# A scheduled RWKV-and-MLP kernel: four buffers of gated values for three, and its list of steps in another order

## The chip, the cores and the metric

The kernel runs on one core of a Trainium2 chip. The metric is the device time of one execution in microseconds (us). The engines have short names here, as in the profile: PE is TensorE (matmuls; PEld is its loading of weights), DVE is VectorE, ACT is ScalarE, POOL is GpSimd, and SP is SyncE, which only issues DMAs. POOL and ACT issue DMAs as well.

## The reference

A linear attention with a decaying state (4 sequences, 8 heads, 768 steps, head size 48) feeds a two-layer MLP with a leaky ReLU (3072 tokens, width 384, inner width 2048). Inputs and output are float32.

```python
for t in range(S):
    kt, vt, rt = (k[:, :, t].copy(), v[:, :, t].copy(), r[:, :, t].copy())
    cur = np.einsum('bhd,bhe->bhde', u[None] * kt, vt)
    y[:, :, t] = np.einsum('bhd,bhde->bhe', rt, state + cur)
    state = w[None, :, :, None] * state + np.einsum('bhd,bhe->bhde', kt, vt)
...
h = x @ w_in
g = np.maximum(0.01 * h, h)
return (g @ w_out).astype(np.float32)
```

## The kernel before

The 3072 tokens are 24 tiles of 128 tokens (n = 0 to 23; six tiles make a sequence). The recurrence is computed tile by tile: inside a tile as a masked product of scores, between the tiles of a sequence through a state. Two tiles make a block (m = 0 to 11) for the MLP.

**The list.** Nothing in the code decides on an order at run time. ORDER (L33) is one string of some 890 step names. The loop at L810 walks it, and each name calls a function that adds one operation to its engine's stream; every engine runs its own steps in the order in which they stand in the list. Sched (L83) works out from what each operation reads and writes which semaphores it waits for. So a step that waits holds up all that stand behind it on the same engine, whether they need it or not. `@` and digits after a name give the PSUM banks that the step opens; a bank can be opened again when its last reader is done.

The steps that are spoken of here, a letter and the number of a tile n or of a block m:

- `k`, `r`, `v` n (L271): load of a tile by POOL, from float32 in DRAM to bf16; `i`, `w`: load of a quarter of the MLP's weights in and out; `p1`: table u; `p9`: a ramp from which the masks are made; other `p`: tables and constants at the start; `p21`: the matmul that spreads w for the tables.
- `P` n (L394): DVE multiplies r and k by tables of powers of w, into qk. `T` n.half (L414): PE transposes it for tiles 0 to 7, and `C` (ACT, L428) copies it out to tp; from tile 8 on `X` n (SP, L408) does it by a DMA transpose.
- `D` (DVE, L434) for tiles 0 to 5, `E`, `f`, `R` (DVE, L439, L445, L450) from tile 6 on: the diagonal term u. `L` n (POOL, L465) lays it into the tile's at buffer by a select.
- `A` n (PE, L473): scores of a tile, into two banks. `M`, `m`, `N` (DVE, ACT, DVE; L487 to L515): mask, into at.
- `K` n (PE, L527): sum of keys times values. `V` (DVE, L557): the diagonal term times v, tiles 0 to 5. `B`, `W` (DVE, L565, L576): the next state st.
- `Y` n (PE, L581): the tile's output. `O` n (ACT, L624): into xT.
- `G` (PE, L633) and `g` (ACT, L648): first MLP product and gate for one tile, four times in block 0. `J` m.j (PE, L656) and `j` m.j (ACT, L670): the same for both tiles of a block and two of 16 column blocks; six matmuls of 256 columns and one activation into gT.
- `t`, `b` (DVE, L707, L719): sums of w_out quarters and of gT blocks. `Z` m.k (PE, L748): one of seven products of eight matmuls of 192 columns each that make the second MLP product of a block from these sums. `z` m.k (ACT or DVE, L772): what is taken out of its bank, added up, into out_sb. `o` n (L696): store of a tile.
- `F` (PE, L382): one filler matmul that nobody reads, in the first 11 us; `q`: a memset.

**Rings.** RINGS (L25) gives the number of buffers of each kind. Its seventh entry, NG, is that of gT, the gated values of a block (L217): block m uses gT[m % NG], and j m.j waits until all readers of the former block in that buffer (its Z and b steps) are done. k and r have ten buffers each, and so has v.

**Where it stands.** The attention runs ahead of the MLP. The first J begins when tiles 0 to 3 are through; from there on J and Z steps make up most of PE's stream, and the attention's steps of later tiles stand between them.

Of the kernel before, what the change touches and what calls it, by code (L numbers as in the profile page):

```python
# [11 lines left out]
B, H, S, D = 4, 8, 768, 48  # L12
L = 128
# [4 lines left out]
E = 64  # L18
# [6 lines left out]
RINGS = (6, 8, 6, 6, 6, 3, 3, 8, 10, 10)  # L25
# [18 lines left out]
f7 J1.5@0 R6 O5 R7 j1.1 K6@7 L6 A7@23 B6 j1.5 A6@45 J2.6@6 j1.4 L7 M6 J2.1@7 k10 J0.5@0 M7 j2.1 J2.4@1 k11 j0.5
b1.0 Y6@7 j2.4 r10 Y7@0 b0.0 J2.5@5 O7 v8 b0.1 O6 J2.7@4 j2.6 b1.1 r11 J2.3@7 j2.7 J2.0@6 j2.5 k13 t0 j2.3
J2.2@0 j2.0 Z0.0@7 b1.2 j2.2 P9 Z0.1@1 z0.0 t1 X9 Z1.0@0 b2.0 J3.1@2 b0.3 Z0.2 P8 Z1.1@3 z0.2 z1.0 t2 X8 z0.1
Z0.3@4 j3.1 J3.3@5 E9 E8 Z0.4 k18 P10 j3.3 f8 K7@6 z1.1 Z1.2 t3 X10 k12 J3.2@2 z1.2 B7 r12 Z1.3@5 f9 E10 r15
z0.4 Z0.5 W7 P11 J3.6@6 r18 f10 X11 z0.5 Z0.6 b1.3 v16 Z1.4 R8 j3.6 E11 J3.7@1 L8 R9 J3.5@6 z1.3 j3.7 R10 r14
# [117 lines left out]
def bass_rwkv5_eagle__then__act_leaky_relu_kernel(  # L166
# [60 lines left out]
    add = sch.add  # L227
# [43 lines left out]
    def load_one(which, n):  # L271
        b, c = divmod(n, NC)
        t0 = c * L
# [596 lines left out]
```

## Time and profile before

| | |
|---|---|
| three runs | 165.57, 164.47, 164.97 us |
| median | 164.97 us |
| profiled execution, its own time | 165.07 us |
| its span, first to last instruction | 163.3 us |
| granted TensorE clock, mean | 1.000 |

| engine | busy us | share of the span | instructions |
|---|---|---|---|
| PE | 154.8 | 95% | 2299 |
| PEld | 137.6 | 84% | 2299 |
| DVE | 130.5 | 80% | 260 |
| ACT | 88.2 | 54% | 194 |
| POOL | 88.1 | 54% | 101 |

Busy time of PE counts a matmul from its start to a modelled end, so that matmuls overlap, and the mean of a matmul in a table of groups is longer than the distance between two. The distance is what PE's time is made of. In the lines of the chain of waits, the second number is the time that the chain spends there, which for back-to-back instructions is that distance.

The busy share in 40 slices of 4.1 us each shows where the engines work; the last line is the share of the DMA engines, in tenths:

```profile
PE   5959999999999698999999999999999999999993
...
DVE  2678978979989999999999999999867770561552
ACT  3486686979443334722795528359057454637120
POOL 7999999996079958999974229223032000000000
...
DMA  6999999999999999999999999900261000005025
```

DVE has hardly a free tenth from 45 to 110 us, the DMA engines until 107 us. POOL's work is for the most part the issuing of loads.

### The profile page before, as it was taken

What the parts mean: (1) busy time and instruction counts of PE and PEld (TensorE: products, weight loads), DVE (VectorE), ACT (ScalarE), POOL (GpSimd) and SP (SyncE); (2) the same over time, 40 slices, a digit from 0 to 9 for tenths busy, and PEclk for the clock granted to TensorE, in tenths of its full rate; (3) what the DMA queues carried; (4) which work ended last, traced back from release to release, by engine and by line L of the source; (5) the groups of instructions that cost most, each with busy time, mean ns of one, the idle gap of its engine ahead of it and who ended that gap; (6) DMA issues with size and microseconds to landing.
All of it is one profiled execution on the core that took longest, in us unless ns stands there. A gap on an engine that the chain in (4) does not pass through costs nothing.

```text
span 163.3 us, 5367 instructions
## 1 busy us (share of the span) xinstructions
PE 154.8 (95%) x2299; PEld 137.6 (84%) x2299; DVE 130.5 (80%) x260; ACT 88.2 (54%) x194; POOL 88.1 (54%) x101
## 2 busy tenths in 40 slices
PE   5959999999999698999999999999999999999993
PEld 1737888888999587999898998989989999999992
DVE  2678978979989999999999999999867770561552
ACT  3486686979443334722795528359057454637120
POOL 7999999996079958999974229223032000000000
PEclk9999999999999999999999999999999999999999
DMA  6999999999999999999999999900261000005025
GB/s 105 137 167 167 154 174 163 186 204 144 145 121 161 100 151 152 130 145 87 150 131 211 264 128 151 230 4 0 62 199 52 0 4 0 0 18 180 4 98 193
DMA packets 100234, 19.89 MB, mean 122 GB/s; under 512 B 93169, under 2 KB 100210, under 8 KB 100210
## 3 DMA queue, kind: packets, MB, share of 16 engines
q0 software_dynamic: 75616, 10.03, 93.8%
q1 hardware_dynamic: 23266, 9.12, 30.4%
q10 hardware_dynamic: 1328, 0.39, 1.0%
q8 instruction: 18, 0.29, 0.7%
q14 instruction: 6, 0.05, 0.1%
HBM read 20.65 MB, written 4.72 MB: 155 GB/s over the span
## 4 chain that ended last, share of the span: by engine, by line
PE 60%; POOL 21%; DVE 9%; DMA 6%; issue 2%; POOLq 0%; DVEq 0%
PE ps_all L766 28%; PE ps_all L664 25%; POOL rk_sb L284 11%; DMA rk_sb<-in_r_dram 6%; POOL v_sb L284 4%; PE ps_all L609 3%; PE ps_all L481 2%; POOL w_out_sb L300 2%; POOL w_in_sb L296 2%; DVE qk L399 2%; DVE at L505 2%; POOL at L467 1%; PE ps_all L539 1%; DVE out_sb L787 1%; DVE s_tok L452 1%
## 5 line engine op out<-in xcount | busy, mean ns | idle before, releaser
L673 ACT ACTIVATE gT<-ps_all 128x512 bf16<-128x512 f32 x92 | 52.0, 604 | 29.3 <-PE ps_all L766 14.1
L664 PE MATMUL ps_all<-xT,w_in_sb 128*128 128x256 bf16 x552 | 66.6, 273 | 0.5 <-DVE at L505 0.5
L664 PEld LDWEIGHTS ps_all<-xT,w_in_sb 128*128 128x128 bf16 x552 | 52.4, 98 | 7.3 <-DVE at L505 0.8
L467 POOL TENSOR_SCALAR_AFFINE_SELECT at<-s_tok 128x1024 bf16<-128x1024 f32 x18 | 20.6, 1155 | 27.0 <-DVE s_tok L452 26.9
L766 PE MATMUL ps_all<-tw,gs 128*128 128x192 bf16 x288 | 28.3, 246 | 0.1
L735 DVE TENSOR_TENSOR gs<-gT 128x1024 bf16<-128x1024 bf16 x24 | 16.1, 686 | 11.1 <-ACT gT L673 5.8
L284 POOL DMA_DIRECT2D rk_sb<-in_k_dram x23 | 21.0, 918 | 7.2 <-DVE ku L442 6.4
L766 PEld LDWEIGHTS ps_all<-tw,gs 128*128 128x128 bf16 x288 | 24.0, 98 | 0.4 <-issue 0.3
L505 DVE CAST_PREDICATED at<-mask,ps_all 128x1024 bf16<-128x1024 uint16 x18 | 21.5, 1216 | 2.0 <-PE ps_all L481 1.8
L284 POOL DMA_DIRECT2D v_sb<-in_v_dram x23 | 21.1, 923 | 0.6 <-PE ps_all L539 0.6
L284 POOL DMA_DIRECT2D rk_sb<-in_r_dram x23 | 21.3, 932 | 0.0
L766 PE MATMUL ps_all<-w_out_sb,gT 128*128 128x192 bf16 x192 | 19.8, 246 | 0.0
L787 DVE TENSOR_TENSOR out_sb<-ps_all,snap 128x192 f32<-128x192 f32 x37 | 12.6, 351 | 5.9 <-PE ps_all L766 5.8
L627 ACT ACTIVATE xT<-ps_all 128x384 bf16<-128x384 f32 x24 | 11.0, 494 | 11.5 <-PE ps_all L609 10.3
L777 ACT ACTIVATE snap<-ps_all 128x192 f32<-128x192 f32 x36 | 11.1, 338 | 11.3 <-PE ps_all L766 10.3
L766 PEld LDWEIGHTS ps_all<-w_out_sb,gT 128*128 128x128 bf16 x192 | 16.1, 98 | 0.5
L399 DVE TENSOR_TENSOR qk<-rk_sb,tab 128x768 bf16<-128x768 bf16 x23 | 13.9, 611 | 2.9 <-DMA rk_sb<-in_r_dram 2.7
L609 PE MATMUL ps_all<-at,v_sb 128*32 128x128 bf16 x384 | 10.4, 220 | 1.1 <-DVE vs L560 1.1
L432 ACT ACTIVATE tp<-ps_all 128x512 bf16<-128x512 f32 x16 | 9.0, 596 | 3.9 <-PE ps_all L421 3.6
L609 PEld LDWEIGHTS ps_all<-at,v_sb 128*32 128x32 bf16 x384 | 8.0, 96 | 3.1 <-DVE vs L560 1.4
L766 PE MATMUL ps_all<-w_out_sb,gs 128*128 128x192 bf16 x96 | 9.9, 246 | 0.0
L782 ACT ACTIVATE out_sb<-ps_all 128x192 f32<-128x192 f32 x11 | 3.7, 332 | 11.3 <-PE ps_all L766 11.3
(69 smaller groups left out, 196.6 us busy)
## 6 DMA issues: line engine op xcount, KB each, us to landing
out_dram<-out_sb SPq DMA_DIRECT2D x22, 192.0 KB, 2.8
rk_sb<-in_k_dram POOLq DMA_DIRECT2D x23, 96.0 KB, 6.0
rk_sb<-in_r_dram POOLq DMA_DIRECT2D x23, 96.0 KB, 6.0
v_sb<-in_v_dram POOLq DMA_DIRECT2D x23, 96.0 KB, 5.5
w_in_sb<-in_moe_w_in_dram POOLq DMA_DIRECT2D x4, 384.0 KB, 6.4
w_out_sb<-in_moe_w_out_dram POOLq DMA_DIRECT2D x4, 384.0 KB, 11.1
tp<-qk SPq DMA_TRANSPOSE x16, 5.2
out_sb<-in_k_dram ACTq DMA_DIRECT2D x1, 192.0 KB, 2.8
```

The lines of the kernel that those rows point to most:

```text
L284: add("pool", lambda: G.dma_start(dst, src), W=[key], dma=f"{which}{n}")
L399: add("dve", lambda: V.tensor_tensor(qk[iq][:, :, 0:D], both, by, ALU.mult), R=[("r", n % NRK), ("k", n % NRK), "qtab", "ktab", ("qk0", iq ...
L467: add("pool", lambda: G.affine_select(out=at[ia][:, :, :, :].rearrange("p two m i -> p (two m) i"), in_=s_tok[i2][:, :].unsqueeze(2).to_br ...
L505: add("dve", lambda: V.copy_predicated(dst, mask[:, :].bitcast(mybir.dt.uint16).unsqueeze(1).to_broadcast([128, H, 128]), raw), R=keys + [ ...
L609: last = PE.matmul(ps_y[32 * q:32 * q + 32, 128 * s:128 * s + 128], a, m, start=first_mm and (s == 0 or whole), stop=last_mm and whole)
L627: add("act", lambda: A.activation(xT[m % NX][:, :, 128 * half:128 * half + 128], ps[i][:, 0:HD].rearrange("p (s t) -> p s t", t=128), AF.C ...
L664: last = PE.matmul(ps[i][:, 256 * f:256 * f + 256], w_in_sb[:, s, 128 * fb:128 * fb + 128], xT[ix][:, s, :], start=s == 0, stop=s == NSL - 1)
L673: add("act", lambda: A.activation(gT[ig][:, 2 * j:2 * j + 2, :].rearrange("p f t -> p (f t)"), ps[i][:, :], AF.Prelu, alpha=0.01), R=[key] ...
L735: add(eng, lambda: on.tensor_tensor(x[i][:, :, :], a, b, op), R=keys, W=[("gs", m % 2, i)])
L766: done = PE.matmul(ps[i][:, 0:NH], lhs[:, s, :], rhs[:, s, :], start=bool(opens) and s == 0, stop=s == HF - 1, skip_group_check=not (opens ...
L777: add("act", lambda: A.activation(snap[i2][j][:, :], ps[i][:, 0:NH], AF.Copy), R=[key], W=[("snap", i2, j)])
L787: add("dve", lambda: V.tensor_tensor(out_sb[io][:, cols], ps[i][:, 0:NH], snap[i2][j][:, :], ALU.add), R=[key, ("snap", i2, j), *after], W ...
```

## The change

NG goes from 3 to 4. A set PAIRED appears, which is empty; load_one can now load two tiles in one DMA for the tiles in that set, and for the others it builds the same pattern from a view with one dimension more. ORDER is replaced: the same steps with the same numbers, but for the fillers (12 instead of 21), in another order and with other banks.

```diff
 VHW = {0}
-RINGS = (6, 8, 6, 6, 6, 3, 3, 8, 10, 10)
+PAIRED = set()
+RINGS = (6, 8, 6, 6, 6, 3, 4, 8, 10, 10)
...
-        t0 = c * L
-        src = {"k": k, "r": r, "v": v}[which][b].rearrange("h t d -> t h d")[t0:t0 + L, :, :]
-        if which == "v":
-            dst = v_sb[:, n % NV, :].rearrange("p (h e) -> p h e", e=E)[:, :, 0:D]
-        else:
-            dst = {"k": k_sb, "r": r_sb}[which][:, n % NRK, :].rearrange("p (h d) -> p h d", d=D)
-        key = (which, n % (NV if which == "v" else NRK))
+        m, slots = (2 if n in PAIRED else 1), (NV if which == "v" else NRK)
+        i = n % slots
+        src = {"k": k, "r": r, "v": v}[which][b].rearrange("h (c t) d -> t c h d", t=L)[:, c:c + m, :, :]
+        dst = {"k": k_sb, "r": r_sb, "v": v_sb}[which][:, i:i + m, :]
+        dst = dst.rearrange("p c (h e) -> p c h e", e=E if which == "v" else D)[:, :, :, 0:D]
+        if m == 1:
+            src, dst = src[:, 0, :, :], dst[:, 0, :, :]
...
-            add("pool", lambda: G.dma_start(dst, src), W=[key], dma=f"{which}{n}")
+            add("pool", lambda: G.dma_start(dst, src), W=[(which, i + j) for j in range(m)], dma=f"{which}{n}")
```

Of the list, which is 44 lines long, these are the stretches that the text speaks of, sorted by engine. POOL, from the start to the last load ahead of L12:

```
before: k1 k2 p9 r1 r2 i1 r3 k3 v1 k5 r5 v2 i0 v3 r4 k4 k7 r7 i3 v4 k6 r6 i2 v7 p1 v5 v6 w0 w1 w3 w2
        k9 r9 v9 r13 k8 r8 L6 L7 k10 k11 r10 v8 r11 k13 k18 k12 r12 r15 r18 v16 L8 r14 v12 L9 k15 L10
        r16 L11 v13 v18 v14 k14 v19 v10 k16 k17 v11 r19
after:  p9 k2 r2 k3 r3 r1 k1 v1 i1 r5 k5 v2 i0 v3 k4 r4 k7 r7 i3 p1 v4 k6 r6 i2 v5 v7 v6 w3 w2 w0 w1
        r9 k9 k8 r8 L6 L7 k10 r10 k13 r11 r13 v13 k11 v8 k20 v9 r15 k12 r12 k15 L8 L9 L10 v15 k18 v16
        L11 k14 v12 v10 r16 k16 v11 r14 r18 k17
```

and, behind L12 and L13, before `k19 k21 v15 r17 k20 v22 r20 r22 v20 r23 v21 L14 r21 k22 L15 L18`, after `k21 k23 v21 k19 r20 r17 k22 r19 v18 L14 L15 r22 L18`.

DVE at the start, from P0.0:

```
before: P0.0 P0.1 P1 P2 p32 D0 M0.1 M0.0 V0 B0 P3 D1 N1.1 M1.0 V1 B1 D2 P5 D3 M3.0 V2 M2 B2 V3 M3.1 P4 M5.0
after:  P0.0 p15 P0.1 p31 P2 D0 P3 q4 p32 M0.1 P1 M0.0 B0 V0 D1 M1.0 q5 N1.1 V1 P5 D2 B1 M2 V2 D3 B2 M3.0
        M3.1 V3 P4 B3 D5 P7 W3 M5.0
```

and from the first t to M10:

```
before: t0 b1.2 P9 t1 b2.0 b0.3 P8 t2 E9 E8 P10 f8 t3 B7 f9 E10 z0.4 W7 P11 f10 z0.5 b1.3 R8 E11 R9 z1.3
        R10 z0.3 P13 f11 B8 z1.4 M8 M9 W8 z1.5 P12 R11 E12 E13 M10
after:  t0 P9 P8 t1 b1.3 P10 t3 E9 E10 P13 f9 f10 b2.0 t2 B7 E8 R9 f8 E11 P11 f11 R8 W7 R10 B8 z0.5 z0.4
        z1.3 z0.3 z1.4 M8 M9 W8 E12 R11 P12 z1.5 M10
```

PE at the start, to the first J:

```
before: F1.256.10@0 F1.256.2@1 p21@7 F1.512.18@6 F1.128.8@5 F1.256.1@6 F1.128.28@0 F1.128.18@1 F1.256.9@2
        F1.256.15@3 F1.256.12@4 F1.128.24@5 F1.256.6@6 F1.256.0@7 F1.512.1@0 F1.256.17@1 T0.0@0 F1.128.25@7
        F1.256.8@6 F1.512.15@7 F1.128.9@1 T0.1@2 F1.512.8@3 T1.1@4 A0@01 T2.1@5 T2.0@6 F1.256.16@7 T1.0@3
        K0@2 Y0@7 A1@01 A2@23 T3.1@4 T3.0@1 K1@5 G0.1@6 Y1@7 A3@01 K2@4 T5.1@5 T5.0@7 G1.1@0 G1.0@7 K3@5
        G0.0@0 Y2@6 Y3@4 T4.1@7 A5@01 T4.0@6 J1.0@2
after:  F1.512.6@0 F1.128.27@1 p21@0 T0.1@7 F1.256.15@6 T0.0@5 F1.512.4@6 F1.512.9@7 T2.1@6 F1.128.30@7
        A0@01 T2.0@7 F1.256.18@2 T3.0@3 F1.512.11@4 F1.512.1@5 T1.1@4 K0@2 T1.0@1 T3.1@0 A1@45 K1@6 Y0@7
        A2@45 Y1@2 G0.1@7 T5.1@1 F1.128.20@0 K2@2 G1.1@6 T5.0@0 F1.128.28@1 F1.128.18@5 A3@34 G0.0@1 G1.0@5
        K3@2 Y2@1 Y3@0 A5@34 T4.0@1 T4.1@2 J1.1@7
```

and from the first Z to the first J4:

```
before: Z0.0@7 Z0.1@1 Z1.0@0 J3.1@2 Z0.2 Z1.1@3 Z0.3@4 J3.3@5 Z0.4 K7@6 Z1.2 J3.2@2 Z1.3@5 Z0.5 J3.6@6 Z0.6
        Z1.4 J3.7@1 J3.5@6 J3.4@5 K8@1 J3.0@7 A8@45 A9@12 Z1.5 Z2.0@6 Z1.6 Y8@4 Y9@5 A10@01 A11@23 Z3.0@7
        J4.4@4 J4.3@5 J4.7@0
after:  Z0.0@5 J2.2@4 Z0.1@3 J3.3@2 J3.4@4 J3.2@0 J3.0@7 J3.1@6 Z1.0@4 Z0.2 Z1.1@0 Z1.2 Z0.3@1 Z0.4 Z0.5
        K8@2 Z1.3@6 Z1.4 A9@23 A8@67 Z1.5 Z1.6 Z0.6 Z2.0@1 Y8@7 Y9@6 A10@23 A11@45 Z3.0@7 J4.6@6 J4.7@0
```

SP's transposes run in the order 9 8 10 11 12 13 15 14 17 18 16 21 22 19 20 23 before, and 8 9 10 11 13 12 15 16 14 21 18 17 22 19 20 23 after; the stores stand between them in both.

More of the change, by code (lines that the diff above doesn't have):

```diff
@@ L44 @@
[L44 to L48, printed above, removed]
@@ new lines @@
+A7@01 L6 j1.4 A6@34 R7 J0.5@5 j0.4 L7 j0.7 M6 J1.5@7 j0.5 J2.1@6 k10 j1.5 M7 K6@2 J2.0@5 r10 J2.6@7 B6 k13 b0.0
+Y6@4 j2.6 Y7@3 b1.0 r11 J2.4@0 O7 b0.1 O6 J2.5@7 r13 j2.0 b1.1 K7@1 j2.4 J2.7@2 b0.2 v13 b0.3 J3.5@0 j2.7 k11 t0
+J2.3@3 j3.5 v8 J3.7@2 P9 j2.3 J3.6@0 j3.7 Z0.0@5 j2.5 P8 j2.1 J2.2@4 t1 X8 Z0.1@3 j2.2 b1.3 J3.3@2 P10 z0.1 X9
+z0.0 J3.4@4 j3.6 t3 J3.2@0 j3.4 E9 E10 J3.0@7 P13 j3.2 k20 X10 f9 J3.1@6 f10 b2.0 v9 Z1.0@4 t2 Z0.2 r15 z1.0 B7
+Z1.1@0 z0.2 k12 j3.1 E8 Z1.2 R9 z1.1 j3.0 f8 r12 Z0.3@1 E11 z1.2 P11 j3.3 Z0.4 k15 f11 X11 R8 Z0.5 W7 L8 R10
```

72 lines of the change are left out of this document (35 added, 37 removed).

## The prediction

> **What bounds the kernel now.** I read the page's head first, then PE's own waits, then PE's busy time by stage.
>
> ```profile
> span 163.3 us, 5367 instructions
> ```
> ```profile
> PE ps_all L481 <- DVE sum_t L573: 1.4, 1, 1.4
> PE ps_all L609 <- DVE vs L560: 1.1, 1, 1.1
> PE ps_all L421 <- DVE qk L399: 0.8, 1, 0.8
> PE ps_all L664 <- DVE at L505: 0.5, 1, 0.5
> ```
> ```profile
> 9.38:22.67 13.29, 11.99 (x275) 9.59 (x276) 11.49 (x24) 9.69 (x21) 13.29 (x17) 1.00 2.16 162
> 22.67:160.64 137.97, 135.91 (x1997) 124.17 (x1994) 114.43 (x217) 74.07 (x166) 66.64 (x72) 1.00 1.18 115
> ```
>
> The stages (length, then busy PE, PEld, DVE, ACT, POOL) say it: from 22.67, where the first two-block matmul group (J1.0) starts, to 160.64, where the last group ends, PE is busy 135.91 of 137.97 us. PE's waits (in total, times, longest) name two of these: 1.4 us at A9 (L481) and 0.5 at J4.7 (L664), both on DVE. The others in the list, and the first filler's, which is not shown, lie ahead of 22.67. So the time is a sum: J start 22.67, PE's fixed work 135.91, its idle 2.06, then 163.30 - 160.64 = 2.66 for the last addition and store, and 165.07 - 163.30 = 1.77 outside the span. Together 165.07, the profiled execution; the median shown, 164.97, is 0.10 lower, which I neglect.
>
> A change of order can't touch 135.91: both lists hold the same J, Z, T, A, K, Y steps, the same ones before the first J, and PE changes as often (35 times) between the small-tile steps (A, Y) and the others behind it. What can move is the start, the 2.06 and, in principle, the tail. A gain is thus capped near 2.06 plus what the start gives; a loss is not capped.
>
> **The fourth buffer.** A gate of block m (j) must wait until the Z steps of block m-3, now m-4, have read its buffer.
>
> ```profile
> ACT gT L673 <- PE ps_all L766: 14.1, 5, 4.7
> ```
>
> That is ACT's wait, 14.1 us of it, and PE's list of waits holds no entry on ACT: ACT has slack there and nobody feels it. Removing it is worth nothing by itself; below nothing isn't to be had either, since no step is longer. It lets the list put all J3 steps ahead of the Z0 steps' end. load_one issues the same descriptors while PAIRED is empty: nothing. Nine filler matmuls fewer (21 to 12): no work that anyone waits for, but see the clock.
>
> **The start.** POOL's loads now begin with ramp, then k2 r2 k3 r3 r1 k1; tile 1's k is the sixth load, not the first.
>
> ```profile
> 8.77 0.56 DVE L399 TENSOR_TENSOR qk<-rk_sb,tab 128x768 bf16<-128x768 bf16 x1 [2.15 <-DMA rk_sb<-in_r_dram]
> 9.48 0.56 DVE L399 TENSOR_TENSOR qk<-rk_sb,tab 128x768 bf16<-128x768 bf16 x1 [0.15 <-DMA rk_sb<-in_r_dram]
> ...
> 10.26 0.43 DVE L436 TENSOR_TENSOR prod<-tp 128x512 bf16<-128x512 bf16 x1
> 10.61 1.28 DVE L491 TENSOR_TENSOR at<-ps_all,mask 128x512 bf16<-128x512 f32 x2
> ```
> ```profile
> 3.77 2.95 PE L387 MATMUL ps_all<-ones 128*128 128x512 bf16 x13
> ...
> 7.80 0.58 PE L421 MATMUL ps_all<-ident,qk 128*128 128x128 bf16 x4
> ...
> 10.66 0.39 PE L421 MATMUL ps_all<-ident,qk 128*128 128x128 bf16 x4
> ...
> 14.78 0.83 PE L642 MATMUL ps_all<-xT,w_in_sb 128*128 128x128 bf16 x12
> 15.63 0.24 PE L609 MATMUL ps_all<-at,v_sb 128*32 128x128 bf16 x4
> ```
>
> The third and fourth loads of today let P1 and P2 start at 8.77 and 9.48, 0.7 apart; so the sixth lands near 9.4 + 2 x 0.7 = 10.8 and P1 ends near 11.4. Then tile 1 goes through its turns, ACT's copies, scores A1, mask, sums and V1 before Y1 can start, as today, where P1 started at 8.77 and Y1 at 15.63, 6.9 later. But today that chain also stood behind P2, D0 and tile 0's masks; in the new list P2, D0, P3 and M0.1 come ahead of P1 while DVE waits anyway. That takes some 2.2 off (P2 0.56, P3 the same, D0 0.43, M0.1 half of 1.28): Y1 at 10.8 + 4.7 = 15.5. From Y1 to the first J PE has the same list as today (15.63 to 22.67, 7.04) and also G0.1, which today runs ahead of Y1 (0.83 with its latency, some 0.7 to the next), less about 0.4 of waits: 7.3. First J at 22.8; with k1's landing read a little early I take 22.75. Bounds: 22.4 if k1 lands 0.4 sooner, 23.2 if the slow fillers just ahead of T1.1 hold it.
>
> These fillers are slow as long as the array is: four transposes took 0.58 at 7.80 and 0.39 at 10.66, so the step to full speed lies between, though the page prints full clock throughout. Today fillers keep PE busy without a break from 3.77, 13 of them in the first row. In the new list hardly any stands between the table matmul and the first turn, and the fillers that are left come behind it, so unbroken work begins near that turn, which today starts as the row's fillers end, at 6.7, 3 us later. If the change comes 3 us later too, it is at 11.4 to 13.7, still ahead of the work from Y1 on.
>
> [...]
>
> **The wait at A9.** Today's 1.39 is the end of a chain on DVE that begins with a load.
>
> ```profile
> 35.97 9.89 DMA rk_sb<-in_r_dram
> ...
> 45.95 0.56 DVE qk L399
> 46.51 0.27 DVE ku L447
> 46.78 0.87 DVE tw L716
> 47.65 0.47 DVE sum_t L573
> ...
> 50.10 0.68 DVE gs L735
> 50.78 0.47 DVE s_tok L452
> ...
> 51.98 0.27 DVE out_sb L787
> ...
> 55.47 0.54 DVE sum_t L573
> ...
> 66.24 1.98 PE ps_all L766 x24
> ```
> ```profile
> 56.07 0.40 PE L481 MATMUL ps_all<-tp 48*128 48x128 bf16 x8 [1.39 <-DVE sum_t L573]
> ```
>
> r10 lands at 45.86, P10 starts, and DVE works with hardly a break to B8, which frees A9's bank at 56.01. In the new list r10 is the sixth load behind the weights, not the ninth; the sixth today is r8:
>
> ```profile
> L284 POOL DMA_DIRECT2D rk_sb<-in_r_dram x1: 1030/1030/1030, 31.1 to 31.1; - x1
> DMA to landing us min/median/max: 12.4/12.4/12.4
> ```
>
> 31.07 + 12.4 = 43.5, so P10, t3, E9, E10 are done near 45.8. P13 comes next and waits for r13, now the ninth load: 45.9 by today's ninth. From its end at 46.5 the new list has, up to z1.3 which frees A8's bank: f9 f10 E8 f8 E11 f11 at 0.27 (1.62), b2.0 0.68, t2 0.87, B7 and B8 0.47 (0.94), R9 R8 R10 at 0.47 (1.41), P11 0.5, W7 0.26, z0.5 z0.4 z1.3 at 0.27 (0.81): 7.1, so 53.6. PE reaches A9 after the same 28 J steps, but with one Z (24 matmuls are three groups, 0.66 each) and one A (0.3) fewer ahead of it: today 56.07 - 22.67 - 1.39 = 32.0 after the first J, now 31.1, at 53.8, and A8 at 54.1. So the wait is covered with 0.5 to spare, and today's second one (J4.7) had DVE's lateness here as its cause. What is late next:
>
> - **POOL's queue.** k20 waits for E10 (45.8); behind it are v9 r15 k12 r12 k15 and the selects L8 L9 L10. Today k18 waits in the same way until 45.92. Six issues of 0.9 end at 51.2, ahead of R8 (51.6), for which L8 waits anyhow; it isn't late. Later v21 waits for Y11, with k19 r20 r17 k22 r19 v18 and L14 L15 behind it; f17, P17 and P19 on DVE may wait for that, and no row prices it: it goes into "the rest" below, from nothing (PE has banks in hand) to 0.5, like today's second wait.
> - **The transposes.** X11 can start near 50.9 (P11), and SP has only X8 to X10 ahead of it:
>
> ```profile
> L410 SPq DMA_TRANSPOSE tp<-qk x16: 1232/1352/2409, 41.2 to 116.9; - x16
> DMA to landing us min/median/max: 3.3/5.2/8.4
> ```
> ```profile
> 59.38 0.62 PE L481 MATMUL ps_all<-tp 48*128 48x128 bf16 x16
> ```
>
>  PE reaches A11 with the same steps done as today (the second of the two in this row, at 59.6, less 1.4 of wait, the start 0.1 later): 58.3. With 5.2 X11 is there at 56.1, with 8.4 at 59.3: 0 to 1.0. With two loads more in front of it than today I take the middle, 0.5.
> - **The selects.** L8, L9 and L10 now run back to back.
>
> ```profile
> 51.16 0.35 DVE L442 TENSOR_TENSOR ku<-rk_sb,u_tab 128x384 bf16<-128x384 bf16 x1
> 51.33 1.14 POOL L467 TENSOR_SCALAR_AFFINE_SELECT at<-s_tok 128x1024 bf16<-128x1024 f32 x1 [0.16 <-DVE s_tok L452]
> ...
> 54.01 1.53 DVE L447 TENSOR_TENSOR ku<-rk_sb,ku 128x384 bf16<-128x384 bf16 x1
> 54.21 1.11 POOL L467 TENSOR_SCALAR_AFFINE_SELECT at<-s_tok 128x1024 bf16<-128x1024 f32 x1
> ```
>
>  f11 met a select and took 1.53 instead of 0.35; E11, which began 0.17 ahead of one, wasn't held. In the new list R8's end starts both W7 and L8, W7 a moment sooner; that is E11's case and I take no cost. Held, W7 would cost DVE 1.2 and A8 0.7.
>
> [...]
>
> So idle behind the first J: 0.5 at A11, 0.2 for the rest (today 0.1 beside the two named), 0.7 in all, between 0.1 and 1.4. The tail keeps its form: Z11.6, z11.6, store o22.0, with two whole-tile stores just ahead on SP as today; no gain or loss.
>
> **Sum:** 22.75 + 135.91 + 0.7 + 2.66 + 1.77 = 163.8, 1.3 below the profiled run.
>
> **Rivals.** *All covered* (0.22): no idle but 0.1 and k1 early: 22.4 + 135.91 + 0.1 + 4.43 = 162.8. For it: DVE has gained at A9. Against: X11's slow case. *r13 late* (0.22): DVE's new list puts P13 ahead of all that A9 and A8 need. Two transposes now start between 42 and 45, ahead of r13's landing, and may push it towards the twelfth load's place:
>
> ```profile
> L284 POOL DMA_DIRECT2D rk_sb<-in_k_dram x1: 918/918/918, 38.6 to 38.6; - x1
> DMA to landing us min/median/max: 11.2/11.2/11.2
> ```
>
>  38.57 + 11.2 = 49.8: P13 ends at 50.4, z1.3 at 57.5, A8 waits 3.4, and with 0.5 elsewhere, today's 2.06 gone and the start's 0.1 the time is 165.07 + 0.1 + 3.9 - 2.06 = 167.0. It is slower than today once r13 lands after about 47.9. *Cold array* (0.08): with 12 fillers for 21 the array stays at half speed until some 17; the 7.3 us of PE work ahead of the first J are then partly done at half speed, 2.2 more (0 to 7): 166.0. For it: fewer fillers. Against: what is left stands behind the first turn without gaps. The forecast has 0.48.
>
> **Numbers.** Faster by over 1% (below 163.3; 1% is about what a measurement of this kernel tells from no change): *all covered* 0.22 and a sixth of the forecast, 0.30. Slower by over 1% (above 166.6): three quarters of *r13 late* and a third of *cold*, 0.20. The rest, 0.50, is within. The range 162.5 to 166.4 leaves out about 0.2; the forecast's own range is 162.9 to 164.7.
>
> **What would show it.** First J between 22.4 and 23.2; no wait at A9 or A8, and J4.7 without one; if PE waits, at A11 with the transpose landing last; P10 no longer waiting beyond 43.6 and P13 near 46; ACT's 14.1 us on Z gone without effect. Wrong would be a PE stall longer than 1 us, above all behind P13, or a first J past 23.5.

## The result: 1.3% slower, and the profile after

| | before | after |
|---|---|---|
| median (lowest to highest) of six runs each | 165.27 us (164.47 to 166.23) | 167.46 us (167.03 to 167.81) |
| profiled execution, its own time | 165.07 us | 167.03 us |
| its span | 163.3 us | 165.3 us |

The ratio after to before is 1.0127, 95% interval 1.0083 to 1.017. The forecast was 163.8 us. In two later sets of runs the changed kernel stood at 1.0175 (1.0126 to 1.0224) and 1.0201 (1.017 to 1.0232) to before.

PE's waits in the changed kernel (in total, times, longest; line numbers behind L25 are one lower than before's here, and one or two lower in the runs below):

```profile
PE ps_all L420 <- DVE qk L401: 2.5, 1, 2.5
...
PE ps_all L663 <- DVE at L504: 1.8, 1, 1.8
PE ps_all L480 <- ACT tp L431: 0.5, 1, 0.5
PE ps_all L480 <- DVE out_sb L786: 0.4, 1, 0.4
...
PE ps_all L765 <- DVE out_sb L786: 0.2, 1, 0.2
```

The waits at A9 and J4.7 are gone. In their place one of 1.8 us stands at a J step, released by an M step; by the order of the steps it is J6.2, which takes bank 3 from M15. The other two behind the first J are at A20 (0.4) and Z5.0 (0.2). The 2.5 and 0.5 lie ahead of the first J. Busy time by stage (length, then busy PE, PEld, DVE, ACT, POOL; the last three numbers are the granted clock, the DMA share and GB/s), first after, then before:

```profile
15.63:23.22 7.59, 7.59 (x198) 6.61 (x194) 7.18 (x15) 4.32 (x10) 7.59 (x10) 1.00 2.05 167
23.22:161.70 138.48, 136.03 (x1997) 124.16 (x1994) 112.92 (x215) 76.18 (x168) 65.76 (x71) 1.00 1.13 114
```
```profile
15.63:22.67 7.04, 6.99 (x178) 5.73 (x179) 5.88 (x12) 4.52 (x9) 7.04 (x9) 1.00 2.13 165
```

Y1 starts at 15.63 in both; the first J at 23.22 against 22.67. From there PE's work is 136.03 (135.91) and its idle 2.45 (2.06). From PE's last end to the end of the span it is 165.30 - 161.70 = 3.60 us (2.66). So the span's 2.0 us are, in these two traces, 0.55 at the start, 0.5 behind it, and 0.9 in the tail. The first of the three is no fixed price: in the nine traces that leave the changed start as it is, the first J came between 23.02 and 23.47, and in the six with before's start between 22.34 and 23.58.

Where the 1.8 us come from is read on DVE and POOL just ahead of 88.85, where J6.2 starts. The timeline of the changed kernel (start, length, operation), DVE and then POOL:

```profile
84.87 0.58 DVE L446 TENSOR_TENSOR ku<-rk_sb,ku 128x384 bf16<-128x384 bf16 x1
85.38 2.28 DVE L398 TENSOR_TENSOR qk<-rk_sb,tab 128x768 bf16<-128x768 bf16 x1
87.58 1.21 DVE L504 CAST_PREDICATED at<-mask,ps_all 128x1024 bf16<-128x1024 uint16 x1
```
```profile
84.10 1.15 POOL L466 TENSOR_SCALAR_AFFINE_SELECT at<-s_tok 128x1024 bf16<-128x1024 f32 x1 [0.75 <-DVE s_tok L451]
85.20 0.92 POOL L283 DMA_DIRECT2D rk_sb<-in_r_dram  x1
86.13 1.11 POOL L466 TENSOR_SCALAR_AFFINE_SELECT at<-s_tok 128x1024 bf16<-128x1024 f32 x1
87.17 0.92 POOL L283 DMA_DIRECT2D v_sb<-in_v_dram  x1
```

P17 (L398) takes 2.28 us; the median of the trace's 23 such steps is 0.55. It ends 0.42 behind the end of the select L18 (86.13 + 1.11 = 87.24). M15 (L504) stands behind it and ends at 88.79. Tile 17's scores aren't due before 100 us, so nobody needs P17 there; it only stands in the way.

The tail is read on SP, whose last stores these are, after and then before:

```profile
160.80 0.33 SPq L703 DMA_DIRECT2D out_dram<-out_sb  x1
161.18 0.92 SPq L698 DMA_DIRECT2D out_dram<-out_sb  x2
162.14 0.89 SPq L703 DMA_DIRECT2D out_dram<-out_sb  x1
```
```profile
159.17 0.33 SPq L704 DMA_DIRECT2D out_dram<-out_sb  x1
159.54 0.93 SPq L699 DMA_DIRECT2D out_dram<-out_sb  x2
161.05 0.33 SPq L704 DMA_DIRECT2D out_dram<-out_sb  x1
```

The last addition, z11.6, takes its 0.36 in both, and o22.0 is issued at once behind it. But it now takes 0.89 us to issue instead of 0.33, and lands 2.7 us after its start instead of 1.8 (after, then before):

```profile
L703 SPq DMA_DIRECT2D out_dram<-out_sb x1: 891/891/891, 162.1 to 162.1; - x1
...
DMA to landing us min/median/max: 2.7/2.7/2.7
```
```profile
L704 SPq DMA_DIRECT2D out_dram<-out_sb x1: 332/332/332, 161.1 to 161.1; - x1
...
DMA to landing us min/median/max: 1.8/1.8/1.8
```

The two whole-tile stores ahead of it, o19 and o21, begin 0.96 us ahead of it; before's pair (o20, o21) 1.5 us. In between, PE ends at 161.70, z11.6 at 162.09.

### The profile page after: what moved, and what is told of

It is laid out like the page before. It is cut to its first block, busy times and chain, and to the rows that moved or that the text cites. A ratio compares the mean times of both kernels' runs of the same rounds, so it can differ in the third digit from the quotient of the medians.

```text
span 165.3 us, 5338 instructions
## 1 busy us (share of the span) xinstructions
PE 154.2 (93%) x2290; PEld 137.2 (83%) x2290; DVE 130.3 (79%) x260; ACT 89.6 (54%) x194; POOL 88.0 (53%) x101
## 4 chain that ended last, share of the span: by engine, by line
PE 83%; DVE 11%; issue 3%; ACT 1%; POOL 0%; DVEq 0%; POOLq 0%
PE ps_all L663 31%; PE ps_all L765 31%; PE ps_all L608 6%; PE ps_all L480 3%; PE ps_all L420 3%; PE ps_all L538 2%; PE ps_all L386 2%; PE ps_all L641 2%; DVE s_tok L451 1%; DVE at L504 1%; DVE gs L734 1%; DVE out_sb L786 1%; DVE qk L398 1%; PE ps_all L612 1%; PE ps_all L319 1%
## 5 line engine op out<-in xcount | busy, mean ns | idle before, releaser
L663 PE MATMUL ps_all<-xT,w_in_sb 128*128 128x256 bf16 x552 | 65.9, 273 | 1.8 <-DVE at L504 1.8
L504 DVE CAST_PREDICATED at<-mask,ps_all 128x1024 bf16<-128x1024 uint16 x18 | 21.5, 1216 | 1.6 <-PE ps_all L480 1.5
L734 DVE TENSOR_TENSOR gs<-gT 128x1024 bf16<-128x1024 bf16 x24 | 16.9, 716 | 7.2 <-PE ps_all L765 5.2
L786 DVE TENSOR_TENSOR out_sb<-ps_all,snap 128x192 f32<-128x192 f32 x37 | 11.9, 349 | 8.2 <-PE ps_all L765 8.2
L398 DVE TENSOR_TENSOR qk<-rk_sb,tab 128x768 bf16<-128x768 bf16 x23 | 14.3, 625 | 1.0 <-PE ps_all L538 0.9
L734 DVE TENSOR_TENSOR gs<-gs,gT 128x1024 bf16<-128x1024 bf16 x12 | 9.8, 825 | 1.4 <-PE ps_all L765 1.2
L451 DVE TENSOR_REDUCE s_tok<-ku 128x8 f32<-128x384 bf16 x18 | 9.7, 545 | 0.2
```

The lines of the kernel that those rows point to most:

```text
L398: add("dve", lambda: V.tensor_tensor(qk[iq][:, :, 0:D], both, by, ALU.mult), R=[("r", n % NRK), ("k", n % NRK), "qtab", "ktab", ("qk0", iq ...
L451: add("dve", lambda: V.tensor_reduce(s_tok[i2][:, :].rearrange("p (two m) -> p two m", two=2), ku[i2][:, :].rearrange("p (m two d) -> p tw ...
L504: add("dve", lambda: V.copy_predicated(dst, mask[:, :].bitcast(mybir.dt.uint16).unsqueeze(1).to_broadcast([128, H, 128]), raw), R=keys + [ ...
L663: last = PE.matmul(ps[i][:, 256 * f:256 * f + 256], w_in_sb[:, s, 128 * fb:128 * fb + 128], xT[ix][:, s, :], start=s == 0, stop=s == NSL - 1)
L734: add(eng, lambda: on.tensor_tensor(x[i][:, :, :], a, b, op), R=keys, W=[("gs", m % 2, i)])
L786: add("dve", lambda: V.tensor_tensor(out_sb[io][:, cols], ps[i][:, 0:NH], snap[i2][j][:, :], ALU.add), R=[key, ("snap", i2, j), *after], W ...
```

## The experiments

Three theories stood for the 1.8 us. **A**: v21 waits on POOL for Y11 (2.47 us), so that r17 is late and P17 with it; the prediction had this queue in view. **B**: the select L18 holds P17. **C**: the issue of the load r22 does. For the tail the theory was the stores ahead of the last one; for the start it was PE's own work, against the fillers. Each diff shows the order of the steps on one engine, without and with the edit. The runs were made in four sets; each ratio is to before in the same set. The changed kernel itself ran again only beside P17's run and in the last set; the other ratios are held against its 1.0127, 1.0175 and 1.0201.

**The buffer alone.** Before's list with four buffers. In it Z5.6 stands behind j9.6, which with four buffers overwrites what it reads, so block 5's last product is made of other values; the operations are the same.

```diff
-RINGS = (6, 8, 6, 6, 6, 3, 3, 8, 10, 10)
+RINGS = (6, 8, 6, 6, 6, 3, 4, 8, 10, 10)
```


> The list of before, word for word, with four buffers of gated values for three. Theory (the buffer is worth nothing by itself, in either direction): same as before, within 0.3% of it; ACT's 14.1 us of waits on Z gone from its list, PE's waits at A9 (1.4) and J4.7 (0.5) still there, first J near 22.7. Rival (the buffer helps because the gates run ahead, or hurts because the gates now collide with other work): off by 0.5 us or more, and then the changed kernel's loss is not the order's alone.

Measured: ratio to before 1.0016 (0.9983 to 1.0049), first J at 22.34. ACT's first and PE's two waits behind the first J:

```profile
ACT gT L671 <- PE ps_all L662: 26.2, 24, 3.4
```
```profile
PE ps_all L479 <- DVE sum_t L571: 1.8, 1, 1.8
...
PE ps_all L662 <- DVE at L503: 0.5, 1, 0.5
```

ACT no longer waits for Z (L764) with a gate, but for J (L662) and, 0.9 in all, for DVE (L733), and PE doesn't notice. The buffer is worth nothing by itself; the loss is the order's.

**v21 out of the way (A against B).**

```diff
-POOL: v21 k19 r20 r17 k22 r19 v18 L14 L15 r22 L18
+POOL: k19 r20 r17 k22 r19 v18 v21 L14 L15 r22 L18
```


> The changed kernel with one load moved on POOL: v21 stands behind v18 instead of ahead of k19, so that k19, r20, r17, k22, r19 and v18 no longer stand behind a load that waits for Y11 (some 2.5 us on POOL). Theory A (the stall of 1.8 us ahead of J6.2 comes of that wait: r17 lands at 84.80 and P17, then M15, are late): r17 lands near 81.5, the stall goes, 1.6 to 2.0 us faster than the changed kernel. Theory B (a select beside it holds P17, which took 2.28 us for 0.55): R14, R15 and R18 set when L14, L15 and L18 run, so these stay where they are, P17 still takes over 1.5 us, the stall stays and the time is within 0.4 us of the changed kernel.

Measured: 1.0117 (1.0043 to 1.019). POOL's wait of 2.5 us is gone and r17 lands at 84.11 (near 81.5 was expected), 3.3 us ahead of P17; yet P17 is held as long, and PE waits 1.7 at J6.2:

```profile
87.39 2.27 DVE L397 TENSOR_TENSOR qk<-rk_sb,tab 128x768 bf16<-128x768 bf16 x1
```
```profile
88.13 1.11 POOL L465 TENSOR_SCALAR_AFFINE_SELECT at<-s_tok 128x1024 bf16<-128x1024 f32 x1
```

A falls. Again P17 ends 0.42 behind the select's end.

**The select out of the way (B against C).**

```diff
-POOL: L15 r22 L18 v19
+POOL: L15 r22 v19 L18
```


> The changed kernel with one select moved on POOL: L18 stands behind v19 instead of ahead of it, so that POOL issues two loads (r22, v19) beside P17 and the select comes 0.9 us later. Theory B (the select holds P17): P17 ends near 85.95 instead of 87.66, M15 near 87.1 instead of 88.8, PE's wait ahead of J6.2 falls from 1.8 to 0.1 to 0.5 us, 1.2 to 1.7 us faster than the changed kernel. Rival C (it is the issue of a load on POOL that holds DVE, since P17 began within r22's issue): P17 still takes 2 us or more, and the time stays. Theory A (r17 late behind v21): r17 lands as late as before, the time stays.

Measured: 1.0038 (1.0002 to 1.0073). POOL and DVE:

```profile
86.76 0.92 POOL L282 DMA_DIRECT2D rk_sb<-in_r_dram  x1
87.67 0.89 POOL L282 DMA_DIRECT2D v_sb<-in_v_dram  x1
88.55 1.12 POOL L465 TENSOR_SCALAR_AFFINE_SELECT at<-s_tok 128x1024 bf16<-128x1024 f32 x1
```
```profile
86.94 0.55 DVE L397 TENSOR_TENSOR qk<-rk_sb,tab 128x768 bf16<-128x768 bf16 x1
87.41 1.21 DVE L503 CAST_PREDICATED at<-mask,ps_all 128x1024 bf16<-128x1024 uint16 x1
```

P17 starts 0.18 into r22's issue as in the changed kernel, and takes 0.55. The stall at J6.2 falls from 1.98 to 0.11. (These two, and the stalls given below, are PE's lag: from the time at which the step ahead would have been through, 88.85 - 86.20 - 0.67 in the changed kernel, some 0.16 more than the wait in the list.) So it is the select, and B stands. In all this trace won less, since loads landed later in it: PE waited 0.65 in all at A9 and A8, which the changed kernel's first trace did not show.

C falls for P17, but not for every step. In before's trace P13 met only load issues on POOL from 52.42 to 54.21, where the next select's recorded start is, and yet took twice its time, which no run here explains:

```profile
52.88 1.21 DVE L399 TENSOR_TENSOR qk<-rk_sb,tab 128x768 bf16<-128x768 bf16 x1
```

**P17 out of the way.** The other half of the pair, beside a further run of the changed kernel:

```diff
-DVE: f17 P17 M15
+DVE: f17 M15 P17
```


> The changed kernel once more, unaltered, as the measure for the three beside it: 0.8 to 1.7% slower than before; in its trace the first J near 23.2, the stall ahead of J6.2 near 1.8 to 2.0 us, 3.6 us from PE's end to the span's end. If its excess over before is spread otherwise than 0.55 (start), 0.52 (stalls, net) and 0.93 (tail), the account of the one trace falls.

> The changed kernel with one step moved on DVE: P17 stands behind M15 instead of ahead of it; POOL's order, L18 among it, is untouched. Theory B (P17 is held by the select beside it, and M15 only stands behind P17): M15 starts at about 85.5 instead of 87.6, isn't held, since it takes 1.21 beside selects elsewhere in the trace, ends near 86.7, PE's wait ahead of J6.2 goes (0 to 0.1 for 1.8), 1.6 to 1.9 us faster than the changed kernel run beside it, less what the next step on DVE gives back. Rival D (M15 would be held in P17's place, or the next A or J step finds the next bank late): wait of 0.8 us or more within the next ten PE steps, less than 1 us gained.

Measured: the changed kernel 1.0175 (1.0126 to 1.0224), with P17 behind M15 1.007 (1.0032 to 1.0108): 1.0%, some 1.7 us by the ratios, 1.55 by the medians (169.05 and 167.5). The stall at J6.2 is gone, though L18 (87.51 to 88.62) lies right beside M15:

```profile
87.07 1.22 DVE L503 CAST_PREDICATED at<-mask,ps_all 128x1024 bf16<-128x1024 uint16 x1 [0.23 <-PE ps_all L479]
88.21 0.83 DVE L397 TENSOR_TENSOR qk<-rk_sb,tab 128x768 bf16<-128x768 bf16 x1
```

M15, one of whose inputs lies in PSUM, isn't held: it takes 1.22, and the eighteen steps of its line in the changed kernel's first trace (L504 there) take 1.21 to 1.23 each, beside a select or not. P17 takes 0.83, and Y15 then waits 0.3 for B15: that is what is given back. In the further run of the changed kernel the first J was at 23.34, the stall 1.84, the tail 3.68, so these three came back. But its ratio lies just above the 0.8 to 1.7% expected, and of the 0.9 us that its span (166.2) is longer than the first trace's these three explain hardly 0.1: the rest isn't accounted for.

**The tail.**

```diff
-SP: o17 o12 o15 o11 o18 o14 o16 o20 o23.0 o19 o21 o22.0
+SP: o17 o12 o15 o11 o14 o16 o18 o19 o20 o21 o23.0 o22.0
```


> The changed kernel with the last whole-tile stores on SP issued as soon as their values are there: o14 behind o11, o16 behind z8.5, o19 behind z9.6, o21 behind z10.6; nothing else is moved. Theory (the last store o22.0 was issued at once when z11.6 ended, but took 0.89 us for 0.33 to issue and landed 2.7 us after its issue for 1.8, behind o19 and o21, issued 1.0 and 0.5 us ahead of it): from PE's end to the span's end 2.7 us instead of 3.60, 0.6 to 0.9 us faster than the changed kernel, with the stall ahead of J6.2 unchanged. Rival (the last store is slow for what ACT's store o22.1, 0.6 us ahead of it, does, as it is in both kernels): within 0.3 us of the changed kernel.

Measured: 1.0063 (1.0022 to 1.0105). This trace's span is 168.4, longer elsewhere (1.9 of it an idle of PE that is told of below), so only the distance from PE's end (165.57) is read: 168.38 - 165.57 = 2.81 instead of 3.60. The last store takes its 0.33 and lands after 1.9:

```profile
L702 SPq DMA_DIRECT2D out_dram<-out_sb x1: 332/332/332, 166.0 to 166.0; - x1
...
DMA to landing us min/median/max: 1.9/1.9/1.9
```

ACT's store o22.1 lies 0.6 ahead as before; it is the stores ahead on SP.

**Fewer fillers.**

```diff
-PE: ... T3.0 F1.512.11 F1.512.1 T1.1 ... T5.1 F1.128.20 K2 G1.1 T5.0 F1.128.28 F1.128.18 A3
+PE: ... T3.0 T1.1 ... T5.1 K2 G1.1 T5.0 A3
```


> The changed kernel without five fillers: F1.512.11 and F1.512.1, which run just ahead of T1.1 (0.43 us apart each), and F1.128.20, F1.128.28, F1.128.18, which stand between Y1 and the first J, where PE is busy 7.59 of 7.59 us (0.1 each). What they compute nobody reads. Theory E (PE is the bound of the start, and fillers in a full stretch cost what they take): first J at 22.5 to 22.9 instead of 23.2, 0.3 to 0.7 us faster. Rival F (the array needs them: without them the step to full speed comes later): transposes still slow (0.6 for 0.39) behind 12.5, first J at 23.2 or later, no gain or a loss.

Measured: 1.0212 (1.0174 to 1.0249); first J at 24.97, 1.75 later than in the first trace. The stalls and the tail are those of the changed kernel. In time the two can't be told apart: the medians are 169.60 and 169.05, and the intervals overlap. PE in the changed kernel, then without the five:

```profile
11.74 0.63 PE L420 MATMUL ps_all<-ident,qk 128*128 128x128 bf16 x4
...
12.47 0.61 PE L420 MATMUL ps_all<-ident,qk 128*128 128x128 bf16 x8
```
```profile
12.55 1.05 PE L419 MATMUL ps_all<-ident,qk 128*128 128x128 bf16 x8
...
17.95 1.11 PE L640 MATMUL ps_all<-xT,w_in_sb 128*128 128x128 bf16 x12
```

Eight transposes take 1.05 instead of 0.61: the array is still at half speed. By the distances, four transposes at 11.71 take 0.41 to the next step, and four at 18.89 take 0.23. It comes to full speed inside the G step that begins at 17.95, which takes 0.94 to the next step, where the one at 19.55 takes 0.67. The trace gives the granted clock as 1.00 from 9.30 to 24.97. So F holds: the five fillers, some 1.1 us of PE (2 x 0.43, and 0.27 for the three), decide on some 6 us of half speed.

**More fillers**: six behind p21, in PE's 2.5 us of waiting.

```diff
-PE: p21 T0.1
+PE: p21 F1.512.20 F1.512.21 F1.512.22 F1.512.23 F1.512.24 F1.256.25 T0.1
```


> The changed kernel with six fillers more (five of 512 columns, one of 256) behind the table matmul p21, where PE waits 2.5 us for the first turn (4.25 to 6.74). Theory (the array of the changed kernel comes to full speed only near 12.4, since PE has gaps ahead of 6.7; busy without a gap from 2 on it comes there near 9 to 10, as before's array does): transposes at 0.39 from about 10 on, T1.1 ends 0.2 to 0.5 earlier, first J at 22.6 to 22.9 instead of 23.2 to 23.4, 0.4 to 0.7 us faster than the changed kernel. Rival (the start is bound by PE's 7.6 us of work behind Y1 and by k1's landing ahead of it, both of which stay): first J within 0.15 us of the changed kernel's.

Measured: 1.0205 (1.0154 to 1.0256). The array is at full speed from 8.6 on (four transposes at 8.59 take 0.39, where those at 11.74 take 0.63 in the changed kernel), 4 us earlier, and the first J is at 23.31 all the same: the rival. PE now waits for P3 and P1, 0.7 each. The changed kernel's array is warm early enough; k1 and PE's work behind Y1 set its start.

**Before's start.** The list of before up to the first J (with its 21 fillers; the expectation counts 20), the changed list from there on:

```diff
-p3 p0 p9 p2 ... T4.0 C4.0 P7 T4.1 J1.1
+p3 p0 q1 k1 ... A5 T4.0 M5.0 J1.1
```


> The changed kernel with the list of before up to the first J (its loads' order, its 20 fillers, its order of turns, scores and masks; banks renamed), and the changed list from there on. Theory (the start costs 0.55 us, and nothing behind it depends on it): first J at 22.3 to 22.7, 0.4 to 0.8 us faster than the changed kernel run beside it; stalls and tail as in the changed kernel. Rival (what is late behind the first J, B3, D5 and the loads from v5 on, eats it up by J6.2): first J early, but the time within 0.2 us of the changed kernel.

Measured: 1.0408 (1.036 to 1.0456). PE's longest wait and its cause on DVE:

```profile
PE ps_all L663 <- DVE at L501: 4.7, 1, 4.7
```
```profile
32.02 0.36 DVE L441 TENSOR_TENSOR ku<-rk_sb,u_tab 128x384 bf16<-128x384 bf16 x1 [5.54 <-DMA u_tab<-in_u_dram]
32.30 1.22 DVE L501 TENSOR_TENSOR at<-ps_all,mask 128x1024 bf16<-128x1024 f32 x1
```

Before loads p1's table late, the changed list uses it early: E7, with M4 behind it. A start can't be exchanged without what relies on it. Its first J came at 23.58; the granted clock was 0.965 on the mean in this trace, and 0.998 with the same start in the second of all mends below, so the clock isn't this start's doing.

**Loads that land late**: in the later traces of the changed start i2, p1 and r13 land later than in the first one, by up to 3.8 us.

```diff
-DVE: E7 M4 E6 V4 P6 B4 V5 W4 b1.2 ... E10 P13 f9 ... P11 f11
+DVE: M4 V4 P6 B4 V5 W4 E7 E6 b1.2 ... E10 f9 ... P11 P13 f11
```


> The changed kernel with three steps of DVE behind what doesn't need their loads: E7 and E6 (which need the table of p1, landing at 23.9 in the first trace and at 24.8 to 27.6 in later ones) behind W4, as in the list of before, and P13 (needs r13, 45.0 in the first trace, 46.8 to 47.5 in later ones) behind P11. Theory (the changed list makes DVE wait for loads with M4 and with z0.5 and z1.3 queued behind it, and so loses 0.3 to 1 us more whenever the loads land later): no wait ahead of J0.7, A9 or A8 whenever the loads land, a spread of the runs as small as before's, 0.3 to 1.0 us faster in the median than the changed kernel's 169.05 of the call ahead (as a ratio to before: 1.0175 falls to 1.010 to 1.015). Rival (J0.4 waits for i2 itself, and the loads cost what they cost): ratio as before, 1.016 or more.

Measured: 1.0165 (1.0114 to 1.0216). The waits at J0.7, A9 and A8 are gone, the time isn't; what these loads cost through DVE is small. But its trace has an idle of 1.5 us at 35.5 that nothing releases, and so has the changed kernel's below.

**All mends**, first with the changed start, then with before's:

```diff
 both: E7 E6 behind W4, P13 behind P11, P17 X17 behind W15, P20 X20 behind z4.5,
       b7.2 behind z6.3, SP's stores as above
+first: the six fillers          +second: before's list up to the first J
```


> The changed kernel with all mends together: the six fillers, E7, E6 and P13 as above, P17 and X17 behind W15 (no step waits behind P17), b7.2 behind z6.3 (so that the select beside it can't delay the drain that A20 waits for), P20 and X20 behind z4.5 (Z5.0), and the last stores as in the run on the tail. Expected by the sum: first J 22.7, 135.9 of work, 0.3 to 0.8 of waits, 2.7 of tail, 1.75 outside the span: 163.4 to 163.9 by the first trace's loads, 164 to 164.7 with later ones, so 0.5 to 1.5% faster than before on the same chip. If a part of the sum doesn't add up (a wait that takes the place of one removed), it is within 0.3% of before or slower.

> The same mends with the list of before up to the first J (its loads and its 20 fillers) in place of the changed kernel's start and of the six fillers; E7 and E6 stand behind W4, so that DVE no longer waits for p1's table (which this start loads last, 32.0 in the run on the start) with M4 behind it. Theory (that run lost its 6 us by E7 ahead of M4, 4.9 at J0.7, and not by the start itself): first J 22.3 to 22.7, no wait at J0.7, 0.3 to 0.6 us faster than the run with the six fillers. Rival (the start of before draws the clock down, 0.56 to 0.59 from 14 to 18 us in that run): first J later than 23, slower than before.

Measured: 1.0068 (1.0029 to 1.0107) and 1.0039 (1.001 to 1.0068). J6.2 and the tail are mended in both; new waits stand at Z5.1 (0.57, P20 now ahead of M16) and A21 (0.68, b7.2 ahead of z6.5), in the second at Y5 (1.1, v5 lands late), in the first the idle at 37. The second's first J came at 22.68 with no wait at J0.7, and its ratio is the lower one, but the intervals overlap.

**What adds up.** Four kernels side by side: start alone, mends alone, both, and the changed kernel.

```diff
 mends: P17 X17 behind W15, P20 X20 behind M16, b7.2 behind z6.5, SP's stores as above
 start: before's list up to the first J, E7 E6 behind W4, Y5 behind J1.4
 both:  mends, start, and P13 behind P11
```


> The changed kernel with only its start replaced by before's (the list up to the first J; E7 and E6 behind W4, Y5 behind J1.4); all behind that is the changed list, its stall ahead of J6.2 and its tail included. Theory G (the changed start costs 0.55 us of PE work and in about half of the executions some 2 us more, since the instructions behind PE's 473rd matmul then come late: the instruction queue's packet at 33 to 34.5 instead of 29.0 to 30.0): the packet at 29 to 30.5, no idle without a releaser, ratio to before 1.005 to 1.012 against 1.0175 of the changed kernel. Rival (that idle is the chip's and not the start's): ratio 1.013 or more, with such idles.

> The changed kernel with its own start, and only the mends behind it: P17 and X17 behind W15, P20 and X20 behind M16, b7.2 behind z6.5, the last stores as in the run on the tail. By the sum of the first trace: 1.9 (J6.2) + 0.25 (Z5.0) + 0.5 (A20) + 0.8 (tail) = 3.4 us off the changed kernel run beside it, so ratio 0.995 to 1.000, if nothing queues up behind the steps moved; 1.005 or more if what is gained at J6.2 is lost again further on.

> All mends, with the waits mended that the last run of this kind showed: the list of before up to the first J, E7 and E6 behind W4, Y5 behind J1.4 (its v5 landed at 31.25 there, 1.1 us late), P13 behind P11, P17 and X17 behind W15, P20 and X20 behind M16 (0.57 at Z5.1), b7.2 behind z6.5 (0.68 at A21), the last stores as in the run on the tail. Expected: first J 22.3 to 22.7, waits 0.3 to 1.0, 2.7 of tail: span 161.5 to 162.6 in the profile, ratio to before 0.985 to 0.994. If a new wait takes the place of these, 0.995 to 1.004.

> The changed kernel once more, as the measure on this chip for the three beside it: ratio to before 1.010 to 1.020; first J 23.1 to 23.5, J6.2's stall 1.8 to 2.0, tail 3.2 to 3.6; where its time goes beyond 167.5, an idle of PE of 1.5 to 2.5 us without a releaser just ahead of its 473rd matmul.

| | ratio to before | 95% interval |
|---|---|---|
| changed kernel | 1.0201 | 1.017 to 1.0232 |
| its start replaced | 1.016 | 1.0119 to 1.0201 |
| the mends behind it | 0.9976 | 0.9945 to 1.0007 |
| both | 0.9953 | 0.9926 to 0.9981 |

The mends are worth 2.2%, 3.4 us by the medians (169.42 and 165.98), as the sum of the first trace had it. The two traces can't confirm the size: the changed kernel's (span 167.3) has an idle of 1.7 that comes next in the text, and that of the mends (162.6) has none. PE's list of waits names none behind the first J any more; PE by stage:

```profile
23.23:159.92 136.69, 136.36 (x1997) 124.08 (x1994) 111.32 (x215) 76.33 (x168) 65.42 (x71) 1.00 1.23 118
```

The start alone brings 0.4%, within the intervals: its first J came at 23.30, where before's trace has 22.67. Theory G, which made the start answerable for 0.55 us and for the late packet, falls as an account of the time: the early packet (29.95) and a trace without the idle came as it said, but the ratio is 1.016 and not 1.005 to 1.012. Both together are 0.5% faster than before and so faster than both kernels.

**The idle without a releaser.** In the changed kernel's last run:

```profile
33.86 0.50 PE L662 MATMUL ps_all<-xT,w_in_sb 128*128 128x256 bf16 x3
36.05 1.16 PE L662 MATMUL ps_all<-xT,w_in_sb 128*128 128x256 bf16 x9 [1.69 <-issue]
```

PE stops in the midst of a J step, three of its six matmuls done, and the profile shows nothing that it waits for. In five traces (tail, more fillers, late loads, the first of all mends, this one) the idle is 1.5 to 2.2 us, and always after exactly 473 matmuls, also where six fillers more put them into another step. The list of DMA queues has an instruction queue, q8. Its packet at that place starts between 33.1 and 35.0 in these five, and between 29.2 and 32.2 in the thirteen others; in the changed kernel's last run it is found from 33 to 34, and in its first one from 29 to 31 (packets, MB, share of the DMA engines):

```profile
q8 instruction: 1, 0.02, 5.6%
```
```profile
q8 instruction: 1, 0.02, 3.0%
```

In the five, PE goes on 2.3 to 2.5 us after the packet's start; in the thirteen others it reaches that matmul 3.1 us or more after it, and does not stop. That PE stands for that packet is the author's reading; it fits all eighteen traces, but it isn't shown: no run moved the packet on purpose, and why it comes late in some is open. It leaves out a shorter idle of 0.66 us without a releaser, after 852 matmuls, in the trace with v21 moved. Open, too, is what of the ratios 1.0175 and 1.0201 beyond the first 1.0127 is due to it.

## Why the prediction was wrong

The range (162.5 to 166.4) missed 167.46. In the profiled execution (167.03) the forecast is exceeded by 3.23: 0.47 at the first J, 0.12 in PE's work, 1.75 in the idle behind it, 0.93 in the tail, less 0.04 outside the span.

- **PE's fixed work untouched**: right in the first trace (136.03 for 135.91). Counted in the lists, the changes between A or Y and the other steps behind the first J are 32 in each, where the prediction has 35; the argument needs only that they are as many.
- **The fourth buffer worth nothing**: right, shown by the run with the buffer alone.
- **The waits at A9 and J4.7 vanish, r10 and P13 in time**: right. The rows of DVE below are P10 (43.6 at the latest was said) and P13 (near 46): r10 landed at 42.86, r13 at 45.04. *r13 late* didn't come true in the first trace; in later ones r13 landed at 45.7 to 47.6 and cost up to 0.65 at A9 and A8, far short of the rival's price.

```profile
43.53 0.55 DVE L398 TENSOR_TENSOR qk<-rk_sb,tab 128x768 bf16<-128x768 bf16 x1
...
45.41 0.55 DVE L398 TENSOR_TENSOR qk<-rk_sb,tab 128x768 bf16<-128x768 bf16 x1
```

- **X11, 0.5 us**: not needed; issued at 50.19 and landed in 5.0, the median's case, and A11 didn't wait.
- **"No row prices it: it goes into 'the rest', from nothing to 0.5"** is the step that failed. It put 0.2 there, and 0.7 for all the idle behind the first J; measured were 2.45, of which 1.8 at J6.2. It named f17, P17 and P19 as what may wait, but because they stand behind v21's wait; that was harmless. What held P17 was L18 beside it, for 1.73 us (2.28 less 0.55), and the assumption that PE has banks in hand failed at M15's bank. A row did price it: the prediction quoted f11 at 1.53 instead of 0.35 beside a select of 1.11, and used it for W7 alone. **W7's case at L8** itself was right, no cost there: W7 took its 0.35.
- **Which step is held** can't be read from a trace's starts: E11 began 0.17 ahead of its select and took its 0.35, f11 began 0.20 ahead and took 1.53, P17 0.75 ahead and took 2.28. P17 was held for 1.73 us beside a select of 1.11, longer than the select itself; no run here shows why.
- **"The tail keeps its form; no gain or loss"** failed for 0.93. The form was kept (two whole-tile stores ahead of o22.0), but their place wasn't looked at: o22.0 came 0.96 us behind them instead of 1.5. The run on the tail shows that this was the cost (2.81 for 3.60).
- **The start, 22.75** was mis-sized, 23.22. 0.13 of it is Y1 (15.63 for 15.5). The rest is in the stretch from Y1 on: 7.59 for 7.3, and PE busy in all of it. The sum had G0.1, but not the three fillers that the list puts there (0.27 by their distances), having called the fillers work that nobody waits for. That they are the reason is argued: the run without them changed the array's speed as well.
- **Cold array** (0.08) was rightly rated low for this list: its array comes to full speed near 12.4 (four transposes at 11.74 took 0.63, eight at 12.47 took 0.61), within the 11.4 to 13.7 that the prediction gave. Five of its twelve fillers less, and the first J comes 1.75 us later (2.2 were said, 0 to 7). Half the speed is what before's distances show (four transposes at 7.80 take 0.42 to the next step, those at 10.66 take 0.22); that it lasts until some 17 with this list, no run shows.

## What to carry to other kernels

Once a list has lost its big waits, look through every pair of a select on POOL and a step on DVE, price each by what such a pair cost in the traces at hand, and ask which PSUM bank stands behind the step on DVE. Here P17 lost 1.73 us beside a select of 1.11, and two E steps of the changed kernel (at 68.00 and 82.18) took 1.53 and 1.38 instead of 0.35 beside selects of 1.18 and 1.16; E11, in before's trace, lost nothing (0.35), nor did the eighteen M steps of L504, which read PSUM (1.21 to 1.23 each). A step that isn't due for long, like P17 here, belongs behind the step that frees a bank. At the end of this kernel, the last store's time hung on when those ahead of it were issued (2.81 us from PE's end instead of 3.60); issue each as soon as its values are there.

## What was not expected of the hardware

- PE stood still for 1.5 to 2.2 us in the middle of a group of matmuls, always after 473 of them, in the five traces in which the packet of the instruction queue started after 33 us, and went on 2.3 to 2.5 us behind that start.
- A DVE step, P17, that started 0.75 us ahead of a select was held by it all the same: it took 2.28 us instead of 0.55 and ended 0.42 behind it (with v21 moved, 0.74 ahead, it took 2.27 and ended 0.42 behind). With the select moved, beside the issue of a load alone, it took 0.55, though before's P13 took 1.21 beside two.
- A store's issue on SP took 0.89 instead of 0.33 us with two others begun in the microsecond ahead of it.
